# Attention and a gated feed-forward layer in one kernel: early weight conversions tied to finished pairs, smaller priority leads, one row scaling moved to ScalarE

## The chip, the cores and the metric

The kernel runs on one core of a Trainium2 chip. The metric is the device time of one execution in microseconds (us), the median of several runs. One further execution was recorded by the hardware profiler. All engines named below belong to that one core: TensorE (PE in the profile; its weight loads are PEld), VectorE (DVE), ScalarE (ACT), GpSimd (POOL), and SyncE (SP), whose queue issues all the DMAs here.

## What is computed

Attention over 32 heads (4 batches of 8 heads, 576 rows, 64 columns), with a linear memory term beside the softmax, then a two-layer feed-forward network with a Mish gate:

```python
scores = where(causal, -1e9, scale * q @ k.T)          # per head
a = exp(scores - max); a /= a.sum + 1e-9
local = a @ v
mem_out = (phi(q) @ M_prev) / (phi(q) @ z_prev + 1e-6) # phi(x) = where(x > 0, x, exp(x) - 1) + 1
attn = g * mem_out + (1 - g) * local                   # g = sigmoid(beta)
x = attn.transpose(0, 2, 1, 3).reshape(2304, 512)
h = x @ w_in                                           # 512 -> 2048
out = (h * tanh(log1p(exp(h)))) @ w_out                # 2048 -> 512
```

The weights `w_in` and `w_out` come in double precision and are turned into pairs of single precision matrices (high and low part) on the chip; `x` and the gated `h` are split in the same way, so each product of the network is three matmuls.

## The kernel before

**Attention, by pairs of heads.** The loop at L515 runs over 16 pairs. A pair goes through these steps. `scores` (L351): TensorE multiplies q by k into a PSUM tile `s` of two banks (L372, eight shapes for a pair); VectorE adds the mask, takes row minima and writes `w` (L382); ScalarE turns each of five row blocks into exponentials (L389). `prep` (L316): phi of q and the memory norm, with one instruction each on VectorE, ScalarE, VectorE and GpSimd and three small ones on VectorE (L321 to L345). `norm` (L406), once for each head: VectorE makes reciprocal sums `rc` (L425, L428), then the five row blocks of `w`, of 64, 192, 320, 448 and 576 columns, are multiplied by `rc` (L432, through `scaled` at L91), and GpSimd puts the memory factor beside them (`cphi`, L410). The string `NRM` at L44 says which engine does each of the five multiplications. `transp` (L440): TensorE transposes `w` block by block into a PSUM tile `t` (L453, 15 for a head), and ScalarE and VectorE in turn copy it into `at` (L457). `av` (L467): TensorE multiplies `at` with `v` into the single PSUM tile `vps` in two halves of 320 and 256 columns (L481); after each half ScalarE copies it to `xo` (L489) and VectorE makes the low part `xl` (L490), called the x operation of the pair below; then both parts go to DRAM (`put`, L492).

**Weight conversion.** `narrow` (L144) turns one 128x512 block of a weight from double precision into a high and a low part: one load into `raw`, of which there is a single buffer in this part (L148), then on VectorE the instructions L155, L161, L164, L171 and a last addition through L89, on ScalarE a scaling (L93) and a cast (L109), and on GpSimd a subtraction (L89). `split` (L184) does this for one block of `w_in` and one of `w_out`. Six of the sixteen blocks are converted during attention; `CV` at L32 says how many behind which pair.

**First part of the network.** From pair 4 on, TensorE also works on the six converted blocks (`steps_a`, L256: first layer in `slot_a`, L226, matmuls at L234; second layer in `out_a`, L241, matmuls at L247, partial sums to DRAM). The rows of `x` it needs are read back from DRAM (`load_x`, L192), four pairs of a batch being needed for a row. This is the filler of TensorE between the attention steps.

**Tail.** When attention has ended, the rest of the filler is merged with the conversion of the other ten blocks, and then the blocks are run over all rows (`tail`, L541, matmuls at L574 and L591).

**What sets the order.** The program is written in one order, and a scheduler puts each engine's instructions into a fixed queue by priority and by its own estimate of when inputs are ready. `run` (L64) can give a group of operations a lead over its place in the text: `OFF` (L75) holds these leads by group, positive for earlier and negative for later. A lead does not change what an instruction waits for, only where it stands in its engine's queue. Each engine then works strictly down its queue.

Of the kernel before, what the change touches and what calls it, by code (L numbers as in the profile page):

```python
# [13 lines left out]
ALU = mybir.AluOpType  # L14
# [14 lines left out]
RP = 5  # L29
P0 = 4  # L30
VB = 2
CV = {1: 1, 3: 1, 4: 2, 5: 1, 6: 1}  # L32
FAE = "avav"
CB = 1
CT = 2
# [5 lines left out]
SPREAD = 2.6  # L41
GPB = 6
TA = 256
NRM = "ppppp"  # L44
ENG = {"ph2": "v", "mghT": "a", "mglT": "v", "min": "v", "zmul": "p", "cphi": "p", "xlo": "v",
       "mgh": "a", "mgl": "v", "wx": "a", "whi": "a", "wsub": "p", "wadd": "v", "wsut": "v", "wadt": "v"}
QT = [(0, 64), (64, 192), (192, 320), (320, 448), (448, 576)]
# [4 lines left out]
def f32(ap):  # L52
    return ap.bitcast(F32)
# [18 lines left out]
            op()  # L72

TC = []
OFF = {'prep1': -400, 'conv': 200, 'av': 100, 'p1': -400, 'scores': 200}  # L75


@with_exitstack
def attention_moe_kernel(ctx: ExitStack, tc: tile.TileContext, f_src, qn, vn, zz, beta, w_in, w_out, out):
    nc = tc.nc  # L80
# [7 lines left out]
    def tt(name, **kw):  # L88
        engines[ENG[name]].tensor_tensor(**kw)  # L89
# [6 lines left out]

    before = [None]

    def queued(ins, chain):
        if chain:  # L100
            tc.add_manual_dep(
                ins.ins, before[0].ins.name,
                mybir.DependencyInfo(mybir.DependencyClass.NoSync, mybir.DependencyReason.DATA), reason="pair",
            )
        before[0] = ins

    def copy(which, o, i):
# [11 lines left out]
    cp = ctx.enter_context(tc.tile_pool(name="cp", bufs=2))  # L119
# [24 lines left out]
    def narrow(pool, own, src, hi, lo):  # L144
        t = {}

        def c0():
            t["r"] = raw = pool.tile([128, 512, 2], I32, tag="raw", name="raw", bufs=1 if own is cp else RT)  # L148
            t["a"] = own.tile([128, 512], I32, tag="e", name="wa", bufs=CB if own is cp else CT)
            t["s"] = own.tile([128, 512], I32, tag="L", name="ws", bufs=CB if own is cp else CT)  # L150
            nc.sync.dma_start(out=raw[:].rearrange("p a b -> p (a b)"), in_=src.bitcast(I32))

        def c1():
            scaled(ENG["wx"], f32(t["a"][:]), f32(t["r"][:, :, 1]), 2.0**-112)
            nc.vector.tensor_scalar(  # L155
                out=t["s"][:], in0=t["r"][:, :, 1], scalar1=-(2**31), scalar2=None, op0=ALU.bitwise_and
            )

        def c2():
            a, s = t["a"], t["s"]  # L160
            nc.vector.scalar_tensor_tensor(  # L161
                out=a[:], in0=a[:], scalar=3, in1=s[:], op0=ALU.logical_shift_left, op1=ALU.bitwise_or
            )
            nc.vector.tensor_scalar(out=s[:], in0=a[:], scalar1=-(2**23), scalar2=None, op0=ALU.bitwise_and)  # L164

        def c3():
            copy(ENG["whi"], hi, f32(t["a"][:]))

        def c4():
            s = t["s"]  # L170
            nc.vector.scalar_tensor_tensor(  # L171
                out=f32(s[:]), in0=t["r"][:, :, 0].bitcast(U32), scalar=2.0**-52, in1=f32(s[:]),
                op0=ALU.mult, op1=ALU.mult,
            )

        def c5():
            tt("wsub" if own is cp else "wsut", out=f32(t["a"][:]), in0=f32(t["a"][:]), in1=f32(hi), op=ALU.subtract)

        def c6():
            tt("wadd" if own is cp else "wadt", out=lo, in0=f32(t["a"][:]), in1=f32(t["s"][:]), op=ALU.add)  # L180

        return [c0, c1, c2, c3, c4, c5, c6]
# [89 lines left out]
    def attention():  # L272
# [194 lines left out]
        def av(p):  # L467
            d = pr[p]
# [17 lines left out]
            def cp(j):  # L486
                q0, n = AVJ[j][0], AVJ[j][1][0][2]
                xo = d["xo"][:, q0:q0 + n]
                copy("a", xo, g_["v", j][:])  # L489
                tt("xlo", out=d["xl"][:, q0:q0 + n], in0=g_["v", j][:], in1=f32(xo), op=ALU.subtract)  # L490

            def put():  # L492
                b, c = divmod(p, 4)
# [3 lines left out]
            g_ = {}  # L497
# [17 lines left out]
        for p in range(NP):  # L515
# [16 lines left out]
            if p >= P0:  # L532
                if (p - P0) % 4 == 0:
                    todo.extend(steps_a((p - P0) // 4))
                n = int(SPREAD * (p - P0 + 1)) - done[0]
# [142 lines left out]
```

## Time and profile before

| | us |
|---|---|
| median of 3 runs | 662.72 (662.42 to 665.02) |
| the profiled execution | 662.44 |
| its span in the trace | 660.7 |
| TensorE busy | 603.4 (91% of the span) |
| VectorE busy | 337.5 (51%) |
| ScalarE busy | 310.7 (47%) |
| GpSimd busy | 167.8 (25%), all of it before the tail |

The span is the time from the first to the last instruction of the program in the trace; the execution's own time is 1.7 us longer. An engine's busy time is the time in which at least one of its instructions ran. The averages over the span mix two stages, attention (up to about 348 us) and tail, so they are read by stretches. "PEclk" is the clock that TensorE was granted, as a share of full speed; in a piece of time it is either 1 (2.4 GHz) or 0.5 (1.2 GHz), and a figure between is a mean over a stretch.

### The profile page before, as it was taken

What the parts mean: (1) busy time and instruction counts of PE and PEld (TensorE: products, weight loads), DVE (VectorE), ACT (ScalarE), POOL (GpSimd) and SP (SyncE); (2) the same over time, 40 slices, a digit from 0 to 9 for tenths busy, and PEclk for the clock granted to TensorE, in tenths of its full rate; (3) what the DMA queues carried; (4) which work ended last, traced back from release to release, by engine and by line L of the source; (5) the groups of instructions that cost most, each with busy time, mean ns of one, the idle gap of its engine ahead of it and who ended that gap; (6) DMA issues with size and microseconds to landing.
All of it is one profiled execution on the core that took longest, in us unless ns stands there. A gap on an engine that the chain in (4) does not pass through costs nothing.

```text
span 660.7 us, 9872 instructions
## 1 busy us (share of the span) xinstructions
PE 603.4 (91%) x3488; PEld 475.2 (72%) x3488; DVE 337.5 (51%) x900; ACT 310.7 (47%) x696; POOL 167.8 (25%) x260
## 2 busy tenths in 40 slices
PE   3577969798979989989989999999999999999997
PEld 2344648576747866757767988888888888888886
DVE  4989898866563654564525888850311211121121
ACT  3677655776763874457923654441222222222221
POOL 3697784465244414543200000000000000000000
PEclk9989988899998999999999999999999999999999
DMA  6344665424441252441418666414302230430230
GB/s 226 103 144 148 203 220 173 124 84 152 151 148 61 96 161 90 141 140 57 141 41 285 204 228 230 136 46 126 114 17 61 94 100 1 129 127 1 64 97 32
DMA packets 50913, 80.86 MB, mean 122 GB/s; under 512 B 8112, under 2 KB 26544, under 8 KB 50864
## 3 DMA queue, kind: packets, MB, share of 16 engines
q1 hardware_dynamic: 50864, 80.24, 37.6%
q8 instruction: 27, 0.44, 0.3%
q14 instruction: 22, 0.18, 0.1%
HBM read 61.35 MB, written 18.87 MB: 121 GB/s over the span
## 4 chain that ended last, share of the span: by engine, by line
PE 50%; ACT 4%; DMA 2%; DVE 1%; POOL 1%; issue 1%; DVEq 0%; ACTq 0%; SPq 0%
PE h L574 19%; PE o L591 19%; PE acc L247 6%; PE h L234 4%; PE vps L481 2%; ACT w L389 1%; PE t L453 1%; ACT L216 1%; DMA raw<-in_w_in_dram 1%; DMA xb<-xs 1%; POOL w L95 0%; ACT L389 0%; ACT g L109 0%; ACT u L216 0%; DVE w L382 0%
## 5 line engine op out<-in xcount | busy, mean ns | idle before, releaser
L89 DVE TENSOR_TENSOR g<-u,g 128x512 fp32r<-128x512 f32 (+1 forms) x77 | 50.7, 667 | 193.8 <-ACT g L109 193.8
L574 PE MATMUL h<-xb,wi 128*128 128x512 f32 (+1 forms) x600 | 134.6, 368 | 0.0
L591 PE MATMUL o<-wo,g 128*128 128x512 f32 x540 | 133.6, 390 | 0.0
L216 ACT ACTIVATE u<-h 128x512 f32<-128x512 f32 (+1 forms) x77 | 43.0, 569 | 169.0 <-PE h L574 164.3
L574 PEld LDWEIGHTS h<-xb,wi 128*128 128x128 f32 x600 | 106.0, 188 | 19.6
L95 POOL TENSOR_SCALAR w<-w,rc 128x64 f32<-128x64 f32 (+4 forms) x160 | 94.6, 616 | 85.6 <-ACT w L389 53.3
L591 PEld LDWEIGHTS o<-wo,g 128*128 128x128 f32 x540 | 100.6, 188 | 20.3
L234 PE MATMUL h<-xb,wi 128*128 128x256 f32 x648 | 100.5, 302 | 8.7 <-DMA xb<-xs 6.8
L389 ACT ACTIVATE w<-w,mx 128x576 f32<-128x576 f32 (+4 forms) x160 | 88.4, 554 | 29.2 <-DVE mx L382 28.9
L234 PEld LDWEIGHTS h<-xb,wi 128*128 128x128 f32 x648 | 88.5, 202 | 17.5 <-DMA xb<-xs 8.2
L372 PE MATMUL s<-f 64*128 64x288 f32 (+4 forms) x384 | 70.6, 480 | 25.7 <-DVE mx L382 18.5
L247 PE MATMUL acc<-wo,g 128*128 128x512 f32 x324 | 83.1, 400 | 5.8 <-ACT g L109 3.5
L453 PE MATMUL t<-ident,w 128*128 128x128 f32 x480 | 74.6, 287 | 7.8 <-ACT at L109 6.3
L372 PEld LDWEIGHTS s<-f 64*128 64x128 f32 x384 | 36.5, 213 | 51.9 <-DVE mx L382 24.4
L247 PEld LDWEIGHTS acc<-wo,g 128*128 128x128 f32 x324 | 59.7, 190 | 19.4 <-ACT g L109 4.0
L453 PEld LDWEIGHTS t<-ident,w 128*128 128x128 f32 x480 | 54.4, 144 | 23.0 <-ACT at L109 7.9
L382 DVE CUSTOM_DVE_ANT_0 w<-s,mask 128x288 f32<-128x288 f32 (+4 forms) x160 | 59.7, 422 | 19.3 <-PE s L372 19.2
L481 PE MATMUL vps<-at,v 128*64 128x256 f32 (+2 forms) x512 | 61.5, 379 | 5.2 <-DVE xl L89 2.7
L481 PEld LDWEIGHTS vps<-at,v 128*64 128x64 f32 x512 | 34.9, 141 | 29.3 <-issue 5.4
L111 DVE COPY at<-t 128x448 f32<-128x448 f32 x64 | 41.5, 649 | 14.3 <-PE t L453 14.3
L93 ACT ACTIVATE wa<-raw 128x512 f32<-128x512 f32 x32 | 21.7, 677 | 52.8 <-DMA raw<-in_w_in_dram 27.3
L109 ACT CAST g<-u 128x512 fp32r<-128x512 f32 (+1 forms) x77 | 44.8, 593 | 1.6
(45 smaller groups left out, 455.9 us busy)
## 6 DMA issues: line engine op xcount, KB each, us to landing
f<-in_f_src_dram SPq DMA_DIRECT2D x32, 288.0 KB, 4.2
xb<-xs SPq DMA_DIRECT2D x36, 256.0 KB, 4.1
raw<-in_w_in_dram SPq DMA_DIRECT2D x16, 512.0 KB, 3.9
raw<-in_w_out_dram SPq DMA_DIRECT2D x16, 512.0 KB, 3.7
qn<-in_qn_dram SPq DMA_DIRECT2D x16, 320.0 KB, 3.0
v<-in_vn_dram SPq DMA_DIRECT2D x16, 320.0 KB, 3.3
xs<-xo SPq DMA_DIRECT2D x16, 288.0 KB, 3.5
xs<-xl SPq DMA_DIRECT2D x16, 288.0 KB, 3.0
```

The costliest lines, as they stand in the source:

```text
L89: engines[ENG[name]].tensor_tensor(**kw)
L95: engines[which].tensor_scalar(out=o, in0=i, scalar1=scale, scalar2=1.0, op0=ALU.mult, op1=ALU.mult)
L216: lambda: nc.scalar.activation(out=u, in_=h, func=ACTF.Mish),
L234: nc.tensor.matmul(ps[:, TA * a:TA * a + TA], wi[y, f][:, c, :], x[c][:, z], start=(q == 0), stop=(q == 11))
L247: nc.tensor.matmul(acc[:], g[:, y, c:c + 128], wo[z, f], start=(f == 0 and y == z), stop=(f == KA - 1 and z == 1),)
L372: nc.tensor.matmul(g["ps"][:, o:o + n], f[le, 0, q0:q0 + 128], f[le, 1, a:b], start=True, stop=True)
L382: nc.vector.tensor_tensor_reduce(out=g["w"][:, WO[m] + D + a:WO[m] + D + b], in0=g["ps"][:, o:o + n], in1=mask[:, c0:c0 + n], scale=-E_SC, ...
L389: nc.scalar.activation(out=row, in_=row, func=ACTF.Exp, scale=-1.0, bias=g["mx"][:, m:m + 1], accum_out=g["sm"][:, m:m + 1])
L453: nc.tensor.transpose(ps[:, o:o + 128], g["w"][:, c:c + 128], ident[:])
L481: queued(nc.tensor.matmul(ps[64 * e:64 * e + 64, a:b], d["v"][:, t, e], at[e][gi][:, c:c + b - a], start=(k == 0), stop=(k == last),), k o ...
L574: nc.tensor.matmul(ps[:, :n], wi[a, f][:, c, :], x[c][:, b], start=(k == 0), stop=(k == 11))
L591: nc.tensor.matmul(D_[t][:], g[:, y, 128 * t:128 * t + 128], wo[z, f], start=(f == KA and y == z), stop=(f == NF - 1 and z == 1),)
```

## The change

Three settings and one ordering rule are changed.

```diff
-CV = {1: 1, 3: 1, 4: 2, 5: 1, 6: 1}
+CV = {0: 1, 1: 1, 3: 1, 4: 1, 5: 1, 6: 1}
-NRM = "ppppp"
+NRM = "ppapp"
-OFF = {'prep1': -400, 'conv': 200, 'av': 100, 'p1': -400, 'scores': 200}
+OFF = {'prep1': 0, 'conv': 0, 'av': 100, 'p1': -400, 'scores': 150}
...
+    done_x = []
+
+    def order_after(ins, first):
+        tc.add_manual_dep(
+            ins.ins, first.ins.name,
+            mybir.DependencyInfo(mybir.DependencyClass.NoSync, mybir.DependencyReason.DATA), reason="order",
+        )
...
-            nc.vector.tensor_scalar(
+            ins = nc.vector.tensor_scalar(
                 out=t["s"][:], in0=t["r"][:, :, 1], scalar1=-(2**31), scalar2=None, op0=ALU.bitwise_and
             )
+            if own is cp and done_x:
+                order_after(ins, done_x[-1])
...
-                tt("xlo", out=d["xl"][:, q0:q0 + n], in0=g_["v", j][:], in1=f32(xo), op=ALU.subtract)
+                ins = nc.vector.tensor_tensor(
+                    out=d["xl"][:, q0:q0 + n], in0=g_["v", j][:], in1=f32(xo), op=ALU.subtract
+                )
+                if j:
+                    done_x.append(ins)
```

The first VectorE instruction of an early conversion (L155) now has to stand behind the second x operation of the last pair that is written before it. Both are on VectorE, so this is an order in the queue and adds no semaphore. The conversion behind pair 0 has no such pair and is free. `prep1` loses its delay, `conv` its lead, and `scores` a quarter of its lead. The 320-column multiplication of every head (32 instructions) goes from GpSimd to ScalarE; the line of the code that writes it is the same, `nrm` at L430. Nothing is computed otherwise than before, and six blocks are still converted during attention.

How the queues change is shown at three places. The lines of the changed kernel stand 7 to 11 higher from L152 on (L155 is L160, L382 is L389, L481 is L488, and the x operation is L497).

VectorE around the second x operation of pair 3 (`xl<-vps,xo 128x256`), before; the number behind `wi_` is the block of the weight that is just finished:

```order
L425 TENSOR_SCALAR rc<-sm,gt 128x5
L341 SCALAR_TENSOR_TENSOR den<-den,gt 128x10
L428 RECIPROCAL rc<-rc 128x5
L89 TENSOR_TENSOR wi_3_92<-wa,ws 128x512
L428 RECIPROCAL rc<-rc 128x5
L345 RECIPROCAL den<-den 128x10
L89 TENSOR_TENSOR xl<-vps,xo 128x256
L155 TENSOR_SCALAR ws<-raw 128x512
```

The same place in the changed kernel:

```order
L89 TENSOR_TENSOR wi_2_88<-wa,ws 128x512
L389 ISA w,mx<-s,mask 128x288
L389 ISA mx 128x1
L389 ISA w,mx<-s,mask 128x288
L389 ISA mx 128x1
L435 RECIPROCAL rc<-rc 128x5
L160 TENSOR_SCALAR ws<-raw 128x512
L168 SCALAR_TENSOR_TENSOR wa<-wa,ws 128x512
L497 TENSOR_TENSOR xl<-vps,xo 128x256
```

Ahead of this x operation VectorE's queue held 35 conversion instructions (seven blocks of five) and now holds 27; ahead of the second x operations of pairs 4, 5, 6 and 7 it held 50, 60, 60 and 60, and now 39, 50, 59 and 60. At the queue's start, four instructions of the first conversion stood ahead of everything else and its fifth ahead of the first L382; now the first of them stands behind four L382. On the SP queue the load of that block's `raw`, which was the first DMA of the program, now stands behind the loads of pair 0's and pair 1's `f` and pair 0's `qn`, `z` and `v`.

TensorE between the second half of `av` of pair 3 and the filler matmul (L234) that needs pair 3's `x`, before:

```order
L481 MATMUL vps<-at,v 64x256 x8
L481 MATMUL vps<-at,v 64x128 x2
L372 MATMUL s<-f 128x288 x2
L453 MATMUL t<-ident,w 128x128 x7
L372 MATMUL s<-f 128x448 x2
L372 MATMUL s<-f 128x64 x2
L453 MATMUL t<-ident,w 128x128 x8
L234 MATMUL h<-xb,wi_0_78 128x256
```

The same place in the changed kernel (L234 is L241):

```order
L488 MATMUL vps<-at,v 64x256 x8
L488 MATMUL vps<-at,v 64x128 x2
L460 MATMUL t<-ident,w 128x128 x7
L379 MATMUL s<-f 128x288 x2
L460 MATMUL t<-ident,w 128x128 x11
L379 MATMUL s<-f 128x448 x2
L379 MATMUL s<-f 128x64 x2
L460 MATMUL t<-ident,w 128x128 x8
L379 MATMUL s<-f 128x320 x2
L379 MATMUL s<-f 128x192 x2
L241 MATMUL h<-xb,wi_0_78 128x256
```

Between the two stood 21 matmuls of pair 4 and 5, and now 36. From the end of pair 15's transposes to the end of the program TensorE's queue is the same in both kernels.

ScalarE behind the 320-column exponentials of pair 2, before:

```order
L389 ACTIVATE w,sm<-w,mx 128x320
L389 ACTIVATE w,sm<-w,mx 128x192
L109 COPY at<-t 128x512
L93 ACTIVATE wa<-raw 128x512
L326 ACTIVATE phe<-phe 128x640
L109 CAST xo<-vps 128x256
L109 COPY at<-t 128x384
L389 ACTIVATE w,sm<-w,mx 128x576 x2
```

The same place in the changed kernel; `w<-w,rc` is the moved multiplication:

```order
L396 ACTIVATE w,sm<-w,mx 128x320
L114 COPY at<-t 128x512
L396 ACTIVATE w,sm<-w,mx 128x192
L114 CAST xo<-vps 128x256
L93 ACTIVATE w<-w,rc 128x320
L114 COPY at<-t 128x384
L93 ACTIVATE w<-w,rc 128x320
L333 ACTIVATE phe<-phe 128x640
L396 ACTIVATE w,sm<-w,mx 128x576 x2
```

The multiplications stand among the copies of transposed blocks and ahead of the next pair's exponentials. ScalarE's queue held 26 loads of activation tables and now holds 24.

## Rows read from the trace of the kernel before

**Rows 1.** The page: the span, and busy us (share of the span) xinstructions by engine.
```profile
span 660.7 us, 9872 instructions
PE 603.4 (91%) x3488; PEld 475.2 (72%) x3488; DVE 337.5 (51%) x900; ACT 310.7 (47%) x696; POOL 167.8 (25%) x260
```

**Rows 2.** Busy time by stretch: us from:to, length, engines, PEclk, DMA share, GB/s.
```profile
0.00:20.00 20.00, 6.90 (x26) 4.07 (x28) 10.55 (x32) 8.56 (x18) 6.50 (x14) 1.00 0.63 217
20.00:92.00 72.00, 54.98 (x358) 34.21 (x354) 65.43 (x209) 44.77 (x132) 57.03 (x77) 0.93 0.48 156
40.00:140.00 100.00, 85.14 (x569) 60.70 (x569) 88.70 (x254) 64.15 (x166) 70.26 (x93) 0.88 0.50 160
92.00:348.00 256.00, 233.92 (x1603) 176.61 (x1601) 147.77 (x464) 163.02 (x380) 104.32 (x170) 0.95 0.38 121
348.00:660.00 312.00, 307.57 (x1506) 260.33 (x1506) 113.74 (x198) 94.37 (x168) 0.00 (x0) 1.00 0.34 110
```

**Rows 3.** Waits of PE: who waited for whom, us in total, times, longest us.
```profile
PE s L372 <- DVE mx L382: 18.5, 12, 4.1
PE s L372 <- DMA f<-in_f_src_dram: 7.0, 1, 7.0
PE h L234 <- DMA xb<-xs: 6.8, 3, 3.2
PE t L453 <- ACT at L109: 6.3, 5, 3.1
PE acc L247 <- ACT g L109: 3.5, 2, 1.8
PE acc L247 <- ACT ob L109: 1.3, 2, 1.0
```

**Rows 4.** Timeline of the first 17 us: start, us, engine, instruction, [idle before <-releaser].
```profile
0.74 0.39 SPq L151 DMA_DIRECT2D raw<-in_w_in_dram  x1
1.18 0.90 SPq L300 DMA_DIRECT2D f<-in_f_src_dram  x2
...
8.86 0.17 DVE L513 TENSOR_SCALAR gt<-gt 128x16 f32<-128x16 f32 x1 [1.85 <-ACT gt L512]
...
9.80 0.68 DVE L89 TENSOR_TENSOR wi<-wa,ws 128x512 fp32r<-128x512 f32 x1
```

**Rows 5.** Groups of VectorE's conversion instructions: xcount | busy us, mean ns | idle before.
```profile
L171 DVE SCALAR_TENSOR_TENSOR ws<-raw,ws 128x512 f32<-128x512 uint32 x32 | 25.1, 785 | 0.5
L161 DVE SCALAR_TENSOR_TENSOR wa<-wa,ws 128x512 int32<-128x512 int32 x32 | 22.9, 715 | 2.3 <-ACT wa L93 2.0
...
L164 DVE TENSOR_SCALAR ws<-wa 128x512 int32<-128x512 int32 x32 | 15.2, 476 | 0.3
...
L155 DVE TENSOR_SCALAR ws<-raw 128x512 int32<-128x512 int32 x32 | 14.2, 443 | 19.7 <-DMA raw<-in_w_in_dram 15.9 <-DMA raw<-in_w_out_dram 3.8
L89 DVE TENSOR_TENSOR wo<-wa,ws 128x512 fp32r<-128x512 f32 x16 | 13.6, 847 | 3.6 <-POOL wa L89 3.5
...
L89 DVE TENSOR_TENSOR wi<-wa,ws 128x512 fp32r<-128x512 f32 x16 | 11.1, 692 | 0.0
```

**Rows 6.** Timeline of PE around the end of pair 3 and the filler's start.
```profile
87.72 3.54 PE L481 MATMUL vps<-at,v 128*64 128x256 f32 x20 [2.04 <-DVE xl L89]
...
98.06 0.39 PE L234 MATMUL h<-xb,wi 128*128 128x256 f32 x1 [1.97 <-DMA xb<-xs]
```

**Rows 7.** PE busy by 5 us: from:to, length, busy (instructions), PEclk, DMA share, GB/s.
```profile
95.00:100.00 5.00, 2.90 (x15) 0.86 0.66 214
100.00:105.00 5.00, 5.00 (x25) 0.50 0.99 321
105.00:110.00 5.00, 5.00 (x39) 0.96 0.15 38
```

**Rows 8.** Groups on ScalarE and GpSimd: the moved scaling and its nearest kin.
```profile
L95 POOL TENSOR_SCALAR w<-w,rc 128x320 f32<-128x320 f32 x32 | 20.0, 624 | 0.0
L389 ACT ACTIVATE w<-w,mx 128x320 f32<-128x320 f32 x32 | 17.8, 558 | 4.6 <-DVE mx L382 4.6
L216 ACT ACT_TABLE_LOAD x13 | 16.7, 1283 | 0.2
L109 ACT CAST xo<-vps 128x320 fp32r<-128x320 f32 x16 | 6.7, 419 | 15.1 <-PE vps L481 15.1
```

**Rows 9.** Waits of GpSimd's scalings for the reciprocal sums.
```profile
POOL w L95 <- DVE rc L428: 23.0, 6, 11.5
```

More of the change, by code (lines that the diff above doesn't have):

```diff
@@ L97, in attention_moe_kernel @@
     before = [None]
+    done_x = []
[4 more added lines that the diff above has]
+        )
     def queued(ins, chain):
         if chain:
[L101 to L104, printed above, removed]
+            order_after(ins, before[0])
         before[0] = ins
```

## The prediction

> **What bounds the kernel now.** I read the page first, then the stretches, then TensorE's waits, then the timelines of the places they point to. The page says TensorE is busy for 91% of the span and every other engine for half or less [rows 1]. That is true of the tail and false of the start, which the stretches show [rows 2]. From 348 us on, TensorE is busy 307.57 of 312 us at full clock; its queue there is the same in both kernels, so this stage moves in time as a block and nothing in it is gained or lost. From 92 to 348 us TensorE has the filler and is busy 233.92 of 256 us. In the first 20 us it is busy for only 6.90 us, and from 20 to 92 us, which is up to the end of pair 3, for 54.98 of 72 us. There VectorE is busy 65.43 of 72 us, or 91%: it is the bound of the first four pairs. TensorE's waits say the same: the largest, 18.5 us in 12 times, is for VectorE's row minima [rows 3]. The first 92 us matter because the filler can't run before pair 3's x is back from DRAM.
>
> So only attention is in play, and the question is when pair 15 ends. The sum is made against the profiled execution of 662.44 us; the median of the three runs is 0.3 us above it, which I add at the end.
>
> **Term 1, the start.** Before, the load of the first weight block goes out first, and the loads that attention waits for follow 0.44 us behind it [rows 4]. It is 512 KB, which at the 217 GB/s of that stretch [rows 2] is 2.4 us of transfer. VectorE's first attention instruction comes at 8.86 us, and the conversion's fifth instruction, 0.68 us, stands ahead of the first row minimum [rows 4]. Without them attention could start between 0 and 3 us earlier. But the conversion's first four instructions ran while VectorE waited for inputs anyway, some 2.5 us that were free and must now be done in the stretch in which VectorE is the bound (they are within the count of term 2). A start up to 1 us worse can't be excluded either, since the second block's load is also queued behind other work. I take **-1 us**, between -3 and +1.
>
> **Term 2, up to pair 3.** Ahead of pair 3's last x operation VectorE now has 27 conversion instructions and not 35. One of the five kinds takes 443, 715, 476, 785 and, for the addition, 770 ns (the mean of 847 and 692) [rows 5], 0.638 us on average, so eight are 5.1 us. With VectorE busy 91% of the time I count 91% of it: **-4.6 us**. If half of this falls into time in which VectorE would be waiting anyway, -2.3; if waits go with it, -5.1. What hides the eight instructions afterwards is the filler: from 92 us on VectorE is busy only 147.77 of 256 us while TensorE has work of its own [rows 2].
>
> **Term 3, pairs 4 and 5.** Ahead of pair 4's last x operation the difference has grown from 8 to 11 instructions, 1.9 us more. Before, the first filler matmul that needs pair 3's x waits 1.97 us for its load at 98.06 us [rows 6], with 21 matmuls put in between; now there are 36, so this wait should be covered. Behind it the clock is at half rate for about one stretch of 5 us [rows 7], up to 3.4 us of lost time if the drop belongs to that wait. From 0 to -7.3 us; I take the first two less a little, **-3.5 us**.
>
> **Term 4, the scaling.** GpSimd loses 32 scalings of 0.624 us, 20.0 us of work [rows 8], in the part of each head that lies between sums and transposes. No wait of TensorE for GpSimd is among its six largest [rows 3], so I count little for that. ScalarE gains 32 instructions that do not stand in the trace. The nearest rows are the 320-column cast, 419 ns, and the 320-column exponential, which also takes a per-row operand and works from and to SBUF, 558 ns [rows 8]; I take the latter, 17.9 us in all, from 13.4 to 17.9. Two table loads of 1.283 us fall away [rows 8], so ScalarE has 15.3 us more. From 20 to 92 us it is busy 44.77 of 72 us, and from 92 to 348 us 163.02 of 256 us [rows 2], so most of it finds room. What doesn't lands on TensorE, whose waits for ScalarE are now 6.3 + 3.5 + 1.3 = 11.1 us [rows 3]. If they grow as ScalarE's load does (15.3 on 216 us up to 348 us, 7%), that is 0.8 us; a burst at each change of pair makes it more. I take **+1.5 us**, from -1 (GpSimd was late somewhere after all) to +8 (half of the new work on the path).
>
> The moved loads cost nothing of their own: the raw blocks now wait in the SP queue behind earlier pairs' releases, but VectorE reaches their first instruction later as well. The order rule adds no semaphore.
>
> Sum: -1 - 4.6 - 3.5 + 1.5 = -7.6, so 662.4 - 7.6 = 654.8, and with the 0.3 us of the median **655.0 us** in round figures. The bounds together would be -16.4 and +6.7.
>
> **The rivals.**
>
> *The gain is given back in pairs 5 to 7.* The ten conversion instructions that are moved behind pair 5 are 6.4 us of VectorE, and the filler of the last two blocks can't start before they are done. If TensorE then waits for them or for the row minima behind them, the sum is -7.6 + 6.4 = -1.2, **661.5 us**. For it: VectorE is busy 88.70 of 100 us from 40 to 140 us [rows 2], so its tightness doesn't end with pair 3. Against it: TensorE has the filler of the first four blocks by then.
>
> *ScalarE takes GpSimd's place (the other side).* GpSimd's scalings stood 23.0 us in six waits for the reciprocal sums [rows 9]. On GpSimd nothing urgent was queued behind them. On ScalarE the copies of transposed blocks and the next pair's exponentials are, so a scaling that waits holds back TensorE's `t` tiles. The whole 17.9 us on the path, in place of the 1.5 I count, would give 655.0 - 1.5 + 17.9 = **671.4 us**. It becomes slower than 666.0 us when more than about 12.5 of these 17.9 us land there, seven in ten. Against it: TensorE waits for ScalarE only 11.1 us in all now [rows 3]. The Trainium skill, "TensorE: Matmul & The Clock Gate", the table at its top, says that ScalarE works strictly first in, first out. By that rule the mechanism of this rival holds; no row here shows an instruction of ScalarE overtaking another.
>
> *TensorE's clock stays up.* From 40 to 140 us the granted clock is 0.88 on average [rows 2]; a share of 0.12 of these 100 us, at a busy share of 0.85, is 10.2 us of matmul time lost to the half rate. If closing TensorE's gaps takes all of it away, the time is 655.0 - 10.2 = **644.8 us**. For it: the 1.2 GHz stretch at 100 us follows a stretch in which TensorE was busy for 2.90 of 5 us, and the clock is back after a full one [rows 7]. Against it: gaps that the change doesn't touch remain, the load of f and the first pairs' chain among them. The Trainium skill, "TensorE: Matmul & The Clock Gate", in its section on HAM oscillation, says that idle stretches let the array fall to half rate and that sustained work brings it back. The trace agrees in kind (0.50 behind 2.90 busy of 5 us); by that rule alone the sum would come out near this rival, and I give it a small chance because the first 92 us stay bound by VectorE.
>
> That the change doesn't do what it says can be left out: the queues show the moves.
>
> **How the numbers follow.** A measurement here can tell a difference of over 0.5%, 3.3 us, from none. Forecast, a gain of 3.3 to 13 us: 0.60. Given back in pairs 5 to 7: 0.20. ScalarE takes GpSimd's place: 0.14. Clock stays up: 0.06. Faster by over 0.5% is forecast and clock, 0.66; the second case is the same, 0.20; the third is slower, 0.14. The range reaches from 645.5 us, near the clock's case, over the given-back case to 664.5 us; it leaves out most of the slower case and the far half of the clock's. The forecast's own range is 649 to 659 us.
>
> **What would show it right or wrong.** The end of pair 3's `av` at 91.3 us (87.72 + 3.54, rows 6) should come 4 to 8 us earlier, with VectorE's busy share up to there unchanged at about 0.9; if it is not earlier, terms 1 and 2 fail. The wait for `xb` of 1.97 us behind pair 3 should be gone; if not, term 3 fails. The new row `w<-w,rc 128x320` on ScalarE should have 32 instructions of 0.42 to 0.56 us, and TensorE's waits for ScalarE should stay under 15 us; over 24 us, the slower rival is right. The stretch from pair 15's end to the end of the program should last as long as before, 314 us within 1 us.

## The result and the profile after

The changed kernel is slower: 668.25 us median of 7 runs (665.38 to 671.46) against 662.42 us (659.99 to 665.02) for the kernel before on the same chip, a ratio of 1.0094 with a 95% interval of 1.0067 to 1.0121. The prediction, 655.0 us in a range of 645.5 to 664.5, missed in sign and in size. The execution in the profile took 669.42 us.

The page of the changed kernel answers to [rows 1]:

```profile
span 667.6 us, 9870 instructions
PE 602.5 (90%) x3488; PEld 472.8 (71%) x3488; DVE 338.7 (51%) x900; ACT 322.4 (48%) x726; POOL 151.2 (23%) x228
```

TensorE's busy time is 0.9 us below that of before and the span is 6.9 us longer, so TensorE stands idle more. Where, the stretches show, cut at the ends of pair 3's and pair 15's `av`. The kernel before (us from:to, length, then busy us and instructions of TensorE, its weight loads, VectorE, ScalarE, GpSimd, then TensorE's granted clock, DMA share, GB/s):

```profile
0.00:91.30 91.30, 61.18 (x380) 37.88 (x380) 75.68 (x238) 52.84 (x148) 62.83 (x90) 0.95 0.51 168
91.30:348.00 256.70, 234.62 (x1605) 177.00 (x1605) 148.07 (x464) 163.51 (x381) 105.02 (x171) 0.95 0.38 122
348.00:660.70 312.70, 307.57 (x1506) 260.33 (x1506) 113.74 (x198) 94.37 (x168) 0.00 (x0) 1.00 0.34 110
```

The changed kernel:

```profile
0.00:92.30 92.30, 60.61 (x379) 37.89 (x380) 70.33 (x228) 55.57 (x153) 54.34 (x79) 0.87 0.48 154
92.30:354.70 262.40, 234.21 (x1605) 174.49 (x1605) 154.75 (x474) 172.32 (x405) 96.81 (x150) 0.96 0.38 123
354.70:667.60 312.90, 307.65 (x1508) 260.42 (x1506) 113.59 (x198) 94.55 (x168) 0.00 (x0) 1.00 0.34 110
```

The tail is the same within 0.2 us. Up to pair 15's end TensorE does the same matmuls with 1.0 us less busy time and 7.7 us more idle time (length less busy time): 30.1 to 31.7 up to pair 3, and 22.1 to 28.2 behind it. In the first stretch VectorE is busy 5.35 us less, as it was meant to be, and the stretch is still 1 us longer: VectorE's own idle time went from 15.6 to 22.0 us. What it waited for there, in the kernel before (who waited for whom, us in total, times, longest us):

```profile
DVE den L340 <- POOL phe L89: 5.1, 4, 2.3
DVE ws L155 <- DMA raw<-in_w_in_dram: 4.4, 1, 4.4
DVE gt L513 <- ACT gt L512: 1.8, 1, 1.8
DVE ws L155 <- DMA raw<-in_w_out_dram: 1.3, 1, 1.3
...
DVE phe L321 <- DMA qn<-in_qn_dram: 0.4, 1, 0.4
```

and in the changed kernel:

```profile
DVE den L347 <- POOL phe L89: 6.7, 2, 4.0
DVE gt L524 <- ACT gt L523: 5.9, 1, 5.9
DVE phe L328 <- DMA qn<-in_qn_dram: 4.1, 3, 1.6
DVE ws L160 <- DMA raw<-in_w_in_dram: 1.6, 1, 1.6
DVE qn L86 <- ACT phe L333: 1.4, 2, 0.9
```

The 5.9 us wait for the gate values is at the very start, but it adds little. Before, VectorE waited there too, for the load of the first conversion and then for the gate values, and worked on that conversion in between; its first row minimum (L382) started at 10.40 us and now starts at 8.14 us. VectorE cut at that point and at pair 3's end (us from:to, length, busy us and instructions of VectorE, TensorE's granted clock, DMA share, GB/s), in the kernel before:

```profile
0.00:10.40 10.40, 3.42 (x7) 1.00 0.66 213
10.40:91.30 80.90, 72.26 (x232) 0.94 0.50 162
```

and in the changed kernel:

```profile
0.00:8.14 8.14, 0.59 (x3) 1.00 0.53 159
8.14:92.30 84.16, 69.74 (x227) 0.86 0.47 153
```

Ahead of the first row minimum VectorE stands idle 7.0 us before and 7.6 us now; behind it, 8.6 and 14.4 us. So 5.8 of the 6.4 us lie behind the first row minimum. Most of them are waits of the feature map's chain: there `den`, the load of `qn` and `qn` behind `phe` take 6.7 + 2.4 + 1.4 us, and before only `den` was waited for, 5.1 us.

TensorE's waits in the changed kernel, which answer to [rows 3]:

```profile
PE s L379 <- DVE mx L389: 19.0, 13, 4.0
PE t L460 <- ACT at L114: 10.2, 9, 3.4
PE h L241 <- DMA xb<-xs: 8.0, 7, 1.8
PE h L241 <- ACT u L223: 4.8, 4, 2.6
PE vps L488 <- DVE xl L497: 4.7, 3, 2.2
PE s L379 <- DMA f<-in_f_src_dram: 4.4, 1, 4.4
PE t L460 <- DVE rc L432: 3.0, 1, 3.0
PE acc L254 <- ACT ob L114: 1.4, 2, 1.1
PE h L241 <- ACT wi L114: 1.1, 1, 1.1
```

The wait for the first load fell from 7.0 to 4.4 us, so attention does start earlier. The waits for ScalarE are 10.2 + 4.8 + 1.4 + 1.1 = 17.5 us; in [rows 3] they were 11.1. The longest is for a copy of transposed blocks of pair 14. TensorE there (start, us, instruction, [idle before <-releaser]):

```profile
326.68 0.66 PE L460 MATMUL t<-ident,w 128*128 128x128 f32 x4
330.72 1.08 PE L460 MATMUL t<-ident,w 128*128 128x128 f32 x4 [3.39 <-ACT at L114]
```

and ScalarE at the same time:

```profile
325.92 1.28 ACT L223 ACT_TABLE_LOAD   x1
327.21 0.60 ACT L223 ACTIVATE u<-h 128x512 f32<-128x512 f32 x1
327.83 1.28 ACT L396 ACT_TABLE_LOAD   x1
329.12 0.67 ACT L396 ACTIVATE w<-w,mx 128x448 f32<-128x448 f32 x1
...
329.79 0.33 ACT L396 ACTIVATE w<-w,mx 128x64 f32<-128x64 f32 x1
...
330.12 0.45 ACT L114 COPY at<-t 128x384 f32<-128x384 f32 x1
```

The transposes end at 327.34 us, and their copy stands behind a second table load and two exponentials of the next pair, to 330.12. The Trainium skill, "TensorE: Matmul & The Clock Gate", the table at its top, has ScalarE work strictly first in, first out; these rows agree with it, the copy waiting 2.78 us behind what stood ahead of it.

### The profile page after: what moved, and what is told of

It reads as the page before. It is cut to its first block, busy times and chain, and to the rows that moved or that the text cites. A ratio compares the mean times of both kernels' runs of the same rounds, so it can differ in the third digit from the quotient of the medians.

```text
span 667.6 us, 9870 instructions
## 1 busy us (share of the span) xinstructions
PE 602.5 (90%) x3488; PEld 472.8 (71%) x3488; DVE 338.7 (51%) x900; ACT 322.4 (48%) x726; POOL 151.2 (23%) x228
## 4 chain that ended last, share of the span: by engine, by line
PE 56%; DMA 2%; ACT 1%; DVE 1%; POOL 0%; issue 0%; SPq 0%; DVEq 0%
PE h L585 18%; PE o L602 18%; PE acc L254 7%; PE h L241 6%; PE vps L488 3%; PE t L460 2%; PE s L379 1%; DMA xs<-xo 1%; DMA xb<-xs 0%; DMA qn<-in_qn_dram 0%; ACT L223 0%; DVE w L389 0%; ACT w L396 0%; POOL phe L89 0%; ACT at L114 0%
## 5 line engine op out<-in xcount | busy, mean ns | idle before, releaser
L89 DVE TENSOR_TENSOR g<-u,g 128x512 fp32r<-128x512 f32 (+1 forms) x77 | 52.7, 691 | 188.1 <-ACT g L114 188.0
L585 PEld LDWEIGHTS h<-xb,wi 128*128 128x128 f32 x600 | 106.0, 188 | 19.6
L241 PE MATMUL h<-xb,wi 128*128 128x256 f32 x648 | 94.8, 294 | 14.8 <-DMA xb<-xs 8.0
L241 PEld LDWEIGHTS h<-xb,wi 128*128 128x128 f32 x648 | 84.1, 194 | 24.2 <-issue 7.8
L95 POOL TENSOR_SCALAR w<-w,rc 128x64 f32<-128x64 f32 (+3 forms) x128 | 74.5, 605 | 103.6 <-DVE rc L435 43.1
L460 PE MATMUL t<-ident,w 128*128 128x128 f32 x480 | 77.9, 293 | 15.1 <-ACT at L114 10.2
L460 PEld LDWEIGHTS t<-ident,w 128*128 128x128 f32 x480 | 55.8, 147 | 32.5 <-issue 20.0
L389 DVE CUSTOM_DVE_ANT_0 w<-s,mask 128x288 f32<-128x288 f32 (+4 forms) x160 | 59.8, 424 | 25.7 <-PE s L379 25.6
L488 PE MATMUL vps<-at,v 128*64 128x256 f32 (+2 forms) x512 | 60.1, 379 | 5.3 <-DVE xl L497 4.7
L488 PEld LDWEIGHTS vps<-at,v 128*64 128x64 f32 x512 | 35.2, 141 | 29.1 <-DVE xl L497 6.2
L114 ACT COPY at<-t 128x384 f32<-128x384 f32 x64 | 33.7, 526 | 24.5 <-PE t L460 24.4
```

The costliest lines, as they stand in the source:

```text
L95: engines[which].tensor_scalar(out=o, in0=i, scalar1=scale, scalar2=1.0, op0=ALU.mult, op1=ALU.mult)
L114: nc.scalar.copy(out=o, in_=i)
L241: nc.tensor.matmul(ps[:, TA * a:TA * a + TA], wi[y, f][:, c, :], x[c][:, z], start=(q == 0), stop=(q == 11))
L389: nc.vector.tensor_tensor_reduce(out=g["w"][:, WO[m] + D + a:WO[m] + D + b], in0=g["ps"][:, o:o + n], in1=mask[:, c0:c0 + n], scale=-E_SC, ...
L460: nc.tensor.transpose(ps[:, o:o + 128], g["w"][:, c:c + 128], ident[:])
L488: queued(nc.tensor.matmul(ps[64 * e:64 * e + 64, a:b], d["v"][:, t, e], at[e][gi][:, c:c + b - a], start=(k == 0), stop=(k == last),), k o ...
```

## The experiments

Eighteen kernels were run, each beside the kernel before on the same chip. The first question was which part of the change carries the loss. Letters in the texts name the theories that each of them states.

**One part alone, added to the kernel before.** First the scaling, then the leads, then the moved conversion with its ordering rule.

```diff
-NRM = "ppppp"
+NRM = "ppapp"
```

> The kernel before with the 320-column scaling on ScalarE alone. Theory S (ScalarE's queue: the scaling holds up the copies of transposed blocks and the exponentials behind it): about 668 us, 5 to 8 us above the kernel before, with TensorE's waits for ScalarE grown from 11.5 us in all to 17 or more. Theory L (the leads put VectorE's reciprocals and copies later): within 2 us of before. Theory C (the conversions, tied to finished pairs, come too late for the filler): within 2 us of before.

Measured: 662.14 us, ratio 1.0015 [0.9992, 1.0038]. The moved scaling alone changes nothing that can be measured.

```diff
-OFF = {'prep1': -400, 'conv': 200, 'av': 100, 'p1': -400, 'scores': 200}
+OFF = {'prep1': 0, 'conv': 0, 'av': 100, 'p1': -400, 'scores': 150}
```

> The kernel before with the three changed leads alone. Theory L: about 668 us, 5 to 8 us above before, with the loss before 92 us, where VectorE's idle time grows. Theories S and C: within 2 us of before.

Measured: 671.33 us, ratio 1.0123 [1.0078, 1.0168]. The leads alone cost at least as much as the whole change. Pair 3's `av` ended only at 101.1 us in this run, against 91.3 us before.

```diff
-CV = {1: 1, 3: 1, 4: 2, 5: 1, 6: 1}
+CV = {0: 1, 1: 1, 3: 1, 4: 1, 5: 1, 6: 1}
+            if own is cp and done_x:
+                order_after(ins, done_x[-1])
```

> The kernel before with the conversions moved (one behind pair 0, one less behind pair 4) and the order rule alone; leads and scaling as before. Theory C: about 668 us, 5 to 8 us above before, lost behind pair 3 where TensorE's filler waits. Theories S and L: at or a few us below before, since the start is 2 us earlier.

Measured: 663.95 us, ratio 1.0020 [0.9997, 1.0043]: no difference shown.

**One part taken out of the changed kernel.** The scaling back on GpSimd:

```diff
-NRM = "ppapp"
+NRM = "ppppp"
```

> The changed kernel with the 320-column scaling put back on GpSimd. Theory S: about 660 us, 6 to 9 us below the changed kernel, with TensorE's waits for ScalarE back at 12 us or less. Theories L and C: within 2 us of the changed kernel, 666 to 670 us.

Measured: 662.76 us, ratio 1.0009 [0.9988, 1.0029]. Here the scaling does seem to matter, by 0.9%, though alone it did not. The three leads as before:

```diff
-OFF = {'prep1': 0, 'conv': 0, 'av': 100, 'p1': -400, 'scores': 150}
+OFF = {'prep1': -400, 'conv': 200, 'av': 100, 'p1': -400, 'scores': 200}
```

> The changed kernel with all three leads put back: the scaling on ScalarE, the moved conversions and the order rule remain. If the scaling costs only where the phi chain already holds up ScalarE's queue (theory Q): 661 to 665 us. If it costs wherever the conversions are moved (their casts and the scalings meet on ScalarE): 667 to 670 us.

Measured: 660.44 us, ratio 0.9993 [0.9970, 1.0016]. Either of two parts taken out removes the loss; the effects do not add. The third part, the moved conversions with their ordering rule, was not taken out alone.

**Which lead.** Each of the three was set alone in the kernel before, and put back alone in the changed one. The feature map's lead alone:

```diff
-OFF = {'prep1': -400, 'conv': 200, 'av': 100, 'p1': -400, 'scores': 200}
+OFF = {'prep1': 0, 'conv': 200, 'av': 100, 'p1': -400, 'scores': 200}
```

> The kernel before with one lead changed alone: prep1 from -400 to 0, which pulls the phi chain of later pairs forward. Theory Q (VectorE's and ScalarE's queues stand at the phi instructions of a later pair, whose qn buffer is reloaded only after an earlier pair's cphi on GpSimd has let go of it): 668 to 672 us, and VectorE's waits for the load of qn grow from 8.1 us to 14 or more. Rival W (the loss of the leads comes from conv and scores, which put conversions and row minima later): within 2 us of before.

Measured: 660.82 us, ratio 0.9982 [0.9960, 1.0005]. The same lead put back in the changed kernel (of the line of leads, only what differs is shown from here on):

```diff
-'prep1': 0
+'prep1': -400
```

> The changed kernel with prep1 put back to -400 alone. Theory Q: 659 to 663 us, 5 us or more below the changed kernel, and pair 3 ends at 88 us or earlier. Rival W: 666 to 670 us, pair 3 at 92 us as in the changed kernel.

Measured: 667.93 us, ratio 1.0085 [1.0061, 1.0109]. Every engine's instructions came in the order of the changed kernel, so this is the same program a second time, and the size of the loss is confirmed. The conversions' lead alone in the kernel before:

```diff
-'conv': 200
+'conv': 0
```

> The kernel before with the lead of conv alone put to 0. Theory V (without its lead a conversion stands behind the next pairs' phi chain and row minima, and the attention chain of the first pairs is longer): 667 to 672 us, pair 3 ends near 100 us. Theory R (the lead of scores is what costs): within 2 us of before.

Measured: 667.76 us, ratio 1.0103 [1.0063, 1.0143]; pair 3's `av` ended only at 101.2 us. In the kernel before, this lead carries most of what the three cost together. The way it does so is not that of the changed kernel, though. Without the ordering rule 44 conversion instructions ran ahead of pair 3's second x operation, where the kernel before has 35 and the changed kernel 27, and VectorE was busy 81.78 us up to pair 3's end instead of 75.68:

```profile
0.00:101.23 101.23, 66.37 (x380) 40.76 (x380) 81.78 (x243) 53.92 (x149) 66.83 (x94) 0.81 0.49 158
```

With all three leads alone it was 44 as well. In these two runs pair 3 ends some 10 us later than before; in the changed kernel it ends 1 us later, and the loss is behind it. The scores' lead alone in the kernel before:

```diff
-'scores': 200
+'scores': 150
```

> The kernel before with the lead of scores alone put to 150. Theory R: 667 to 672 us. Theory V: within 3 us of before.

Measured: 664.45 us, ratio 1.0044 [1.0015, 1.0074], a small loss. The conversions' lead put back in the changed kernel:

```diff
-'conv': 0
+'conv': 200
```

> The changed kernel with the lead of conv alone put back to 200. Theory V: 659 to 663 us, with the order rule keeping the conversions behind finished pairs. Theory R: 666 to 670 us.

Measured: 658.31 us, ratio 0.9945 [0.9920, 0.9970], faster than both kernels, with the instructions of the changed kernel on the same engines but for two more loads of activation tables on ScalarE. The scores' lead put back in the changed kernel:

```diff
-'scores': 150
+'scores': 200
```

> The changed kernel with the lead of scores alone put back to 200. Theory R: 659 to 663 us. Theory V: 666 to 670 us.

Measured: 660.05 us, ratio 0.9971 [0.9946, 0.9995]. This lead put back also removes the whole loss, so the two theories, each of which named one lead as the cause, both see their number come true, and neither lead alone is the cause.

One guess at what a lead does was that the phi loads wait for their buffer, of which there are two. The leads alone, with a third buffer:

```diff
-            d["qn"] = ap_.tile([128, 5, 2, D], F32, tag="qn", name="qn")
+            d["qn"] = ap_.tile([128, 5, 2, D], F32, tag="qn", name="qn", bufs=3)
```

> The kernel before with the three changed leads and a third buffer for qn. Theory Q: the wait for the reload goes, so 660 to 665 us, against 671 with the same leads and two buffers. Rival P (the phi chain costs by its place in the queues alone, whatever its input does): 668 to 672 us.

Measured: 668.85 us, ratio 1.0100 [1.0067, 1.0133], and pair 3's end at 103.1 us instead of 101.1. The buffer was not it.

**Every queue pinned.** So far each edit let the scheduler make a new order, so an edit's own cost and that of the new order could not be told apart. In the next four kernels every queue is written out as it stands in the changed kernel, by a chain of ordering rules, and one thing is altered by hand. No kernel was run with the chain alone; the second of the four, at 667.30 us, shows that the chain itself costs little.

```diff
+    for n in ORDER:
...
+        if last is not None and ins[last].engine == ins[n].engine:
+            tc.add_manual_dep(
+                ins[n], ins[last].name,
+                mybir.DependencyInfo(mybir.DependencyClass.NoSync, mybir.DependencyReason.DATA), reason="order",
+            )
+        last = n
```

First the 32 scalings out of ScalarE's queue into GpSimd's; nothing else changes place (one head shown).

```diff
 ScalarE
-L93 ACTIVATE w<-w,rc 128x320
 GpSimd
+L95 TENSOR_SCALAR w<-w,rc 128x320
 L95 TENSOR_SCALAR w<-w,rc 128x448
```

> The changed kernel with every queue written out as it stands there, and only the 32 row scalings of 320 columns taken out of ScalarE's queue and put into GpSimd's, each just ahead of the 448-column scaling of its head. Theory E (what costs is the time of the scaling in ScalarE's queue, 32 x 0.56 = 17.6 us): the loss against the kernel before goes, 660 to 664 us, as with the scaling on GpSimd and the order left to the scheduler (ratio 1.001). Theory O (what costs is the order that the scheduler made, and the scaling matters only by the order that follows from it): as the changed kernel, 667 to 671 us, ratio 1.008 to 1.014, TensorE's waits for ScalarE's copies still there behind pair 3.

Measured: 678.56 us, ratio 1.0272 [1.0245, 1.0299]. With the order held, and with this place in GpSimd's queue, the scaling on ScalarE is not the loss but a gain of some 1.8%. The figure holds for this exchange only: the rest of the order was made for the scaling on ScalarE, and the run doesn't part ScalarE's relief from a later GpSimd. TensorE's wait for ScalarE's copies stayed as it was, at 9.9 us for 10.2:

```profile
PE t L460 <- ACT at L114: 9.9, 8, 3.5
```

This kernel and the one with the scaling back and a free order (ratio 1.0009) hold the same instructions on the same engines, but for two loads of activation tables that this one has less. Their order in the queues sets them 2.6% apart. Up to pair 15's end the pinned one:

```profile
0.00:96.40 96.40, 65.24 (x379) 41.03 (x380) 70.64 (x229) 51.57 (x144) 59.90 (x89) 0.81 0.46 147
96.40:360.70 264.30, 235.64 (x1605) 177.40 (x1605) 153.87 (x474) 161.64 (x383) 107.99 (x172) 0.95 0.38 122
```

and the one with the free order:

```profile
0.00:93.20 93.20, 61.78 (x380) 38.64 (x380) 73.69 (x230) 51.48 (x144) 60.59 (x89) 0.93 0.48 156
93.20:346.90 253.70, 229.47 (x1607) 172.55 (x1605) 155.15 (x473) 164.63 (x384) 112.30 (x172) 0.97 0.39 126
```

The larger part of the difference is TensorE's busy time for the same matmuls, 9.6 us longer up to pair 15's end at a lower granted clock, 0.81 against 0.93 in the first stretch; its idle time is 4.2 us longer.

Then the three longest waits of TensorE for ScalarE behind pair 3, taken out by moving four instructions of ScalarE's queue.

```diff
+L223 ACTIVATE u<-h 128x512 x2
 L93 ACTIVATE wa<-raw 128x512
 L114 CAST wi<-wa 128x512
-L223 ACTIVATE u<-h 128x512 x2
...
-L333 ACTIVATE phe<-phe 128x640
 L114 COPY at<-t 128x512
+L333 ACTIVATE phe<-phe 128x640
...
+L114 COPY at<-t 128x384
 L223 ACTIVATE u<-h 128x512
 L396 ACTIVATE w,sm<-w,mx 128x448
 L396 ACTIVATE w,sm<-w,mx 128x64
-L114 COPY at<-t 128x384
```

> The changed kernel with every queue written out as it stands there, and only three places of ScalarE's queue mended, where TensorE waits longest for it behind pair 3: the two Mish of pair 6's stretch ahead of the weight conversion's two operations (wait of 2.62 us), the copy of pair 6's transposes ahead of the exp of pair 9's feature map (2.60 us), the copy of pair 14's transposes ahead of a Mish and its table load (3.39 us). Sum 8.6 us. Theory O, with these three places as what costs: 660 to 664 us, ratio 0.998 to 1.004, the three waits under 1 us each. Rival D (the waits only show a chain over all engines that is late anyway; taken away in one place they come back in another): 666 to 669 us, ratio above 1.006, with other waits grown in their stead.

Measured: 667.30 us, ratio 1.0100 [1.0076, 1.0124]. The waits for `at` fell, others grew, and nothing was won:

```profile
PE s L379 <- DVE mx L389: 22.4, 14, 4.8
...
PE t L460 <- ACT at L114: 4.5, 7, 1.4
...
PE h L241 <- ACT wi L114: 3.0, 1, 3.0
```

Rival D holds for these three: each wait was where a delay showed, and not what made it.

Then less work for VectorE ahead of pair 3, in an unchanged order.

```diff
+        k = slice(0, 16 if thin else 512)
-                out=t["s"][:], in0=t["r"][:, :, 1], scalar1=-(2**31), scalar2=None, op0=ALU.bitwise_and
+                out=t["s"][:, k], in0=t["r"][:, k, 1], scalar1=-(2**31), scalar2=None, op0=ALU.bitwise_and
```

Here `thin` holds for the first five halves; L168, L171 and L178 are cut in the same way, and the last addition reads `wa` in place of `ws`. A half is the one block of `w_in` or of `w_out` that `narrow` converts; the thin instructions leave out 496 columns of each, in three weight blocks.

> The changed kernel with every queue written out as it stands there; of the five weight halves that are converted ahead of pair 3's x operation, four of VectorE's five operations work on 16 columns instead of 512 (20 instructions, about 13 us of VectorE's time less; the low and high words of three weight blocks are left wrong). If VectorE's work bounds the first four pairs, as the prediction had it, pair 3's last matmul ends at 79 to 84 us instead of 92.3. If a chain through all engines bounds them, with VectorE only one link of it, it ends at 87 to 91. If VectorE's work there is covered altogether, at 91.5 or later.

Measured: 661.77 us, ratio 1.0010 [0.9983, 1.0037]. Pair 3's `av` ends at 85.4 us instead of 92.3:

```profile
83.21 2.17 PE L493 MATMUL vps<-at,v 128*64 128x256 f32 x20 [1.27 <-DVE xl L502]
```

VectorE is busy 62.90 us up to there instead of 70.33:

```profile
0.00:85.40 85.40, 59.95 (x379) 37.91 (x380) 62.90 (x228) 55.05 (x153) 51.12 (x79) 0.94 0.51 166
```

So 7.4 us less work brings 6.9 us at pair 3's end, and the ratio falls from 1.0094 to 1.0010. The result lies between the two numbers expected, because the thin instructions saved less than the 13 us assumed (by the means of [rows 5] the 20 take only 12.1 us at full width); by the share that was won, VectorE's work does lie on the path. Still, this kernel only draws level with the kernel before: its stretch behind pair 3 takes 259.9 us, where the kernel before takes 256.7.

Last, the first weight half converted at the start again, as in the kernel before.

```diff
 DMA queue
+L156 DMA raw<-in_w_in_dram 128x1024
 L307 DMA f<-in_f_src_dram 128x576 x2
 VectorE
+L160 TENSOR_SCALAR ws<-raw 128x512
+L168 SCALAR_TENSOR_TENSOR wa<-wa,ws 128x512
+L171 TENSOR_SCALAR ws<-wa 128x512
+L178 SCALAR_TENSOR_TENSOR ws<-raw,ws 128x512
 L524 TENSOR_SCALAR gt<-gt 128x16
```

> The changed kernel with every queue written out as it stands there, and only the conversion of the first weight half moved to the start, as it stands in the kernel before: its load ahead of pair 0's on the DMA queue, four of its five VectorE operations at the head of VectorE's queue, into the time in which VectorE waits for pair 0 anyway (7.6 of the first 7.7 us), the fifth behind pair 0's first feature map operation; its ScalarE and GpSimd operations ahead of pair 0's. Theory H (conversions ran in time that was idle before; the change moved them among work that is waited for): pair 3's last matmul ends at 88 to 91.5 us instead of 92.3 to 93.6, the time is 663 to 666 us, ratio 1.003 to 1.007. Rival N (the later scores of pair 0, about 2.6 us, eat it up, or the idle time comes back elsewhere): pair 3's end at 92 us or later, ratio 1.008 or more.

Measured: 670.51 us, ratio 1.0136 [1.0107, 1.0164], pair 3's end at 93.8 us. It did not fill the hole. VectorE's second conversion instruction waited for ScalarE:

```profile
8.20 0.69 DVE L168 SCALAR_TENSOR_TENSOR wa<-wa,ws 128x512 int32<-128x512 int32 x1 [3.42 <-ACT wa L93]
```

I had put ScalarE's part of the conversion behind the two exponentials of the gate, and the experiment tests theory H only in that form. The traces above say what the start of the kernel before is worth: its first row minimum came 2.3 us later than in the changed kernel, with 2.8 us more of VectorE's work done.

**A version that beats both.** The kernel with the conversions' lead put back, once more:

> The changed kernel with the lead of the conversions alone put back to 200, once more and in more rounds: 657 to 660 us, ratio 0.992 to 0.997, if the first measurement holds; 0.997 or more if it was chance.

Measured: 657.10 us, ratio 0.9935 [0.9911, 0.9959]. With the scores' lead put back too:

```diff
-OFF = {'prep1': 0, 'conv': 0, 'av': 100, 'p1': -400, 'scores': 150}
+OFF = {'prep1': 0, 'conv': 200, 'av': 100, 'p1': -400, 'scores': 200}
```

> The changed kernel with the leads of the conversions and of the scores put back to 200 (the lead of the feature map at 0, the order rule, the moved conversion and the scaling on ScalarE stay). If the gains of the two leads put back one at a time (0.55% and 0.3% against the kernel before) add: 655 to 657 us, ratio 0.990 to 0.993. If each only gives another order, with no sum: 658 to 663 us, ratio 0.995 to 1.003.

Measured: 660.33 us, ratio 0.9979 [0.9956, 1.0002]: two settings that each help do not add. The version with the one lead put back is the best found. Its stretches:

```profile
0.00:92.00 92.00, 62.07 (x383) 38.41 (x384) 74.19 (x237) 58.61 (x160) 56.37 (x85) 0.86 0.49 158
92.00:341.30 249.30, 226.92 (x1601) 171.16 (x1601) 151.53 (x466) 172.92 (x400) 92.06 (x144) 0.98 0.40 129
```

It ends pair 3 at about the same time as the kernel before and the changed one, with VectorE busy 74.19 us by then, and the next stretch is 13 us shorter than in the changed kernel, 5.8 us less idle time of TensorE and 7.3 us less busy time for the same work, at a granted clock of 0.98. Against the kernel before, TensorE's idle time in that stretch is the same (22.4 us for 22.1), and what is gained is busy time for the same matmuls, 226.92 us for 234.62 at 0.98 for 0.95. Why this order has the higher clock is not shown.

## Why the prediction was wrong

The sum missed in two places of about the same size. Up to pair 3's end, terms 1 and 2 came to -5.6 us, and it came 1.0 us later. From there to pair 15's end, terms 3 and 4 came to -2.0 us, and the stretch grew by 5.7 us.

**What bounds the kernel.** The tail moved as a block: 312.9 us against 312.7, as said (the 314 us named for it is the execution's 662.4 us less 348, and the trace's span is 1.7 us shorter). That VectorE's work bounds the first four pairs held in kind: with the order fixed, 7.4 us less of it brought 6.9.

**Term 1, the start.** Right as far as it went: TensorE's wait for its first load is 2.6 us shorter (4.4 us instead of the 7.0 of [rows 3]). VectorE's first row minimum came 2.3 us earlier, and the 2.8 us of conversion that had been done by then moved behind it, as the term said.

**Term 2, up to pair 3, is the first step that failed.** The work was removed as counted: the trace has 27 conversion instructions ahead of pair 3's last x operation instead of 35 (25 instead of 35 by the end of its `av`), and VectorE's busy time fell by 5.35 us. The step "With VectorE busy 91% of the time I count 91% of it" took the idle time as given, though. It belongs to the order, and the order was changed: idle time rose by 6.4 us, 5.8 of them behind the first row minimum and most of these waits of the feature map's chain, and pair 3 ended at 92.3 us instead of the 83 to 87 predicted. Had term 2 come true, the kernel would still not have been faster: in the run with less work in the same order pair 3 ended at 85.4 us, and the time was that of the kernel before. The statement that VectorE's share would stay near 0.9 up to there fails as well, at 70.33 of 92.30 us, or 0.76. The share of before, from the start on, was 0.83; the 0.91 was taken from a stretch that left the idle start out.

**Term 3, pairs 4 and 5, failed.** The wait for pair 3's `x` was still there, 1.84 us for 1.97 [rows 6]:

```profile
100.78 1.14 PE L379 MATMUL s<-f 64*128 64x320 f32 x8 [1.76 <-DVE mx L389]
...
104.51 1.73 PE L241 MATMUL h<-xb,wi 128*128 128x256 f32 x9 [1.84 <-DMA xb<-xs]
```

A single filler matmul went ahead of it at 101.84 us. The 36 matmuls put in between, instead of 21, waited themselves, 1.76 us for row minima among others, and did not cover it. Counting matmuls in a queue says nothing of how long they take. The larger miss here is what no term stood for: the new order made the whole stretch from pair 3 to pair 15 longer, by 6.1 us of TensorE's idle time.

**Term 4, the scaling.** The price of one scaling was right:

```profile
L93 ACT ACTIVATE w<-w,rc 128x320 f32<-128x320 f32 x32 | 17.6, 558 | 5.9 <-DVE rc L435 5.7
```

What it does to the time has no one value. Alone in the kernel before it cost 0.15%, some 1.0 us, which can't be told from none or from the +1.5 us of the term; put back on GpSimd with a new order, it took 0.9% off the changed kernel, and put back in the same order it added 1.8%. TensorE's waits for ScalarE reached 17.5 us, over the 15 and under the 24 that were named.

**The rivals.** The slower rival, "ScalarE takes GpSimd's place", gave 671.4 us, and the time came near it, by luck: taking the scaling off ScalarE in the same order made it slower still, and left TensorE's wait for the copies as it was. "The gain is given back in pairs 5 to 7" saw that something would be given back, but nothing was gained up to pair 3, and what was lost behind it came on top. The clock's rival came in part, and without its gain: from 40 to 140 us the granted clock was 0.95 where it had been 0.88 [rows 2], and TensorE's busy time there fell from 85.1 to 81.3 us with 12 matmuls more:

```profile
40.00:140.00 100.00, 81.32 (x581) 57.26 (x577) 83.73 (x238) 68.89 (x173) 56.50 (x73) 0.95 0.50 160
```

The rival that was missing is that new settings make a worse order by themselves. The text treated the leads as what moves the conversions, and gave their effect on every other instruction no case. Run alone, they cost 1.2%.

What is shown: the loss comes from the order in the queues, since the conversions' lead put back, with the same instructions on the same engines but for two table loads more, is 1.5% faster than the changed kernel. It hangs on no single setting: the scaling, the conversions' lead or the scores' lead put back alone each removes all of it, and the feature map's lead has no part. It appears as idle time: of VectorE up to pair 3, where it eats the gain, and of TensorE behind it. In the six executions that have the changed kernel's order on TensorE (the changed kernel, its repeat and the four with queues written out) TensorE stood idle 25.4 to 28.7 us from pair 3's end to pair 15's, against 22.1 us before and 21.9 to 24.9 us in the five versions of the changed kernel with another order. What stays open is which places of which queues make this idle time. Three likely ones on ScalarE were mended without gain.

## What to carry to other kernels

Where a scheduler makes the queues, an edit is two edits, its own cost and a new order, and the second was the larger here. Pinning the queues prices the first, but for that one order. A high busy share told rightly here that VectorE's work was on the path, but its idle time belonged to the order, so the work taken away counted only where the waits stayed put. A long wait in a list need not be a new one: the 5.9 us at the start stood in place of two waits of before. And an early milestone is not the end: pair 3 ended 6.9 us earlier in one run, and the kernel only drew level.

## What was unexpected of the hardware

VectorE instructions on 16 columns had two prices. Those kinds take 443 to 785 ns on 512 columns [rows 5]. Of the 20 thin ones, 14 took 158 to 176 ns each, and six took 309 to 901 ns. GpSimd was at work during each of the six slow ones, on a product or a difference of two tensors in five of them; it was also at work during five of the 14 fast ones, on a scaling by a column of factors in four. One kind, fast and slow, the second with GpSimd's instruction that ran beside it (start, us, engine, line, instruction):

```profile
14.57 0.18 DVE L182 SCALAR_TENSOR_TENSOR ws<-raw,ws 128x16 f32<-128x16 uint32 x1
...
58.38 1.54 POOL L90 TENSOR_TENSOR phe<-qn,z 128x640 f32<-128x640 f32 x1
...
59.05 0.90 DVE L182 SCALAR_TENSOR_TENSOR ws<-raw,ws 128x16 f32<-128x16 uint32 x1
```

So the thin kinds' means, 217 to 405 ns, say little of either sort. That GpSimd's work slows VectorE's is what the rows suggest; no run here sets out to test it.

TensorE's clock also differs between two executions of one program: the changed kernel was granted 0.87 up to pair 3, and its repeat, with the same queues, 0.92 up to 93.6 us, with busy times of 60.61 and 61.18 us. A difference of one or two us between single profiles is therefore read as nothing here; the loss behind pair 3 has that uncertainty too, being 6.1 us of idle time in the one and 4.5 us (26.6 less 22.1) in the other.
